# Two recurrent chains rebuilt: output sums of all heads in one PSUM bank, weights in groups of 160 columns, padded memory keys, short waits filled with products

## The chip, the cores and the metric

One core of one Trainium2 chip. The metric is the device time of one execution in microseconds (us). The engines: PE multiplies matrices and adds up in PSUM; DVE (vector), ACT (scalar) and POOL copy and compute; SP only issues transfers (DMA), as POOL does too; SBUF is the memory on the chip. Engines wait for each other by semaphores, counters that a finished instruction or transfer raises.

## The reference

The kernel computes the forward pass and all gradients of a gated mix of two blocks. Block A (multi-query attention) isn't touched. Block B is an attention that carries a memory: 64 segments of 32 tokens, each with 8 memory rows in front, 32 heads of 128; the outputs of the memory rows are the next segment's memory. Cut to what matters:

```python
for s in range(n_seg):                                   # 64, one after the other
    h = jnp.concatenate([mem, xs], axis=1)               # 8 memory rows + 32 tokens, 576 wide
    q, k, v = (jnp.einsum('btd,dhe->bhte', h, W) for W in (Wq, Wk, Wv))
    p = _softmax(where(mask, einsum('bhqe,bhke->bhqk', q, k) * scale, -1e9))
    o = jnp.einsum('bhqk,bhke->bhqe', p, v)
    o = jnp.einsum('bhte,hed->btd', o, Wo)               # sums over all heads
    mem = o[:, :M, :]                                    # the chain
    outs.append(o[:, M:, :])
out = g * a + (1 - g) * b                                # and the gradients by jax.vjp
```

The tokens' rows can be worked on 128 at a time. The memory rows can't: they make a forward chain of 64 segments and, for the gradient, a backward chain of 64.

## The kernel before

A segment of the forward chain, from the normalised outputs to the next memory:

```python
rl = sp.tile([P, 2, 1], F32, name="c_rl", bufs=2)
nc.vector.reciprocal(rl[:, :, 0], po[:, 2, 0:2])          # 256 reciprocals of the softmax sums
nc.vector.tensor_tensor(out=oc[:], in0=po[:, 0:2, :], in1=rl[:].to_broadcast([P, 2, P]), op=ALU.mult)
nc.gpsimd.dma_start(self.RL_m[s].rearrange("r p -> p r"), rl[:, :, 0])     # kept for the backward chain
# ... stores of ET, OM, ME, OT on POOL; transposes of oc; copy to oT ...
pw = psum.tile([P, 640], F32, name="c_pw", bufs=1)
for ri in range(8):                                       # 4 heads side by side: 64 products
    for lo, hi in ((0, 512), (512, D)):
        for g in range(4):
            self.mm(pw[32 * g:32 * g + 32, lo:hi], lhsT=oT[:, c0:c0 + 32], rhs=WoN[:, h, lo:hi],
                    start=(ri == 0), stop=(ri == 7), tp=(0, 32 * g))
ws = sp.tile([P, 640], F32, name="c_ws", bufs=1)          # two engines copy pw to ws, in f32
for kt in range(NKT):                                     # sum the 4 row groups, turn rows to columns
    self.mm(pm[:, kt, :], lhsT=ws[:, kt * P:(kt + 1) * P], rhs=self.selF[:, :], start=True, stop=True)
nc.vector.tensor_copy(mT[:, :, (s + 1) * MEM:(s + 2) * MEM], pm[:, :, :])
```

The backward chain has the same projection three times a segment (for v, k and q, with the transposed weights `WT`, 64 products each) and the same tail. `WT` is loaded before the backward chain and serves the x gradients too.

The softmax here doesn't subtract the row's maximum and nothing guards it: scores larger than these inputs give would overflow.

## Time and profile before

| | us | clock |
|---|---|---|
| time, median of 3 runs | 11834.84 (11804.16 to 11844.51) | 0.697 |
| forward chain | 1423 | 0.81 |
| x attention | 1510 | 0.77 |
| backward chain with its loads | 1150 | 0.88 |
| wait before the x gradients | 13 | |
| x gradients | 969 | 0.74 |
| memory rows | 118 | 0.51 |
| weight gradients | 687 | 1.00 |

The stages are cut at the first and last product of each on PE (the matmul engine); the first 5938 us (block A, projections, weight transposes) are left out. Clock is the mean share of full speed that PE was granted. The lines of the profile that carry this are in the prediction below.

### The profile page before, as it was taken

The page shows a single profiled execution, that of the slowest core. Times are in us where ns is not written, and L with a number is a line of the kernel's source. Part 1 is how long each engine was busy: PE and PEld are TensorE (multiplying, and loading weights), DVE is VectorE, ACT ScalarE, POOL GpSimd, SP SyncE. Part 2 cuts the span into 40 slices and gives each one's busy share as a digit, 9 for nine tenths or more (in the row PEclk, how much of TensorE's full clock was granted, in tenths as well). Part 3 has the DMA queues.
Part 4 walks back from the last instruction along what each step waited for, and adds up shares of the span by engine and source line. Part 5 has one row for each costly group of instructions (what it writes and reads, how often), then busy time and mean ns, then how long its engine had stood idle before and what let it go on. Part 6 is the DMA issues. An engine that isn't in the chain of part 4 may idle for free. (4 is left out here: it accounts for less than half of the span.)

```text
span 11807.0 us, 189310 instructions
## 1 busy us (share of the span) xinstructions
PE 10704.6 (91%) x79411; PEld 4101.3 (35%) x79798; DVE 4365.5 (37%) x6102; ACT 3510.0 (30%) x4681; POOL 2793.4 (24%) x5477
## 2 busy tenths in 40 slices
PE   7999999999999999989888888888887888999799
PEld 2212121212121212134433333555544554555444
DVE  4555555555555555534311111333332222122200
ACT  3444444444444444423311111222221111111100
POOL 3000000000000000013245555333334444333100
PEclk8555555555555555589888877777778988777799
DMA  2000000000000000045532222555544333555544
GB/s 66 1 4 1 4 1 4 1 4 1 4 1 1 4 1 1 1 144 231 201 83 54 54 55 70 190 174 167 176 152 149 90 93 94 186 188 187 192 147 145
DMA packets 583499, 980.07 MB, mean 83 GB/s; under 512 B 213801, under 2 KB 392114, under 8 KB 564402
## 3 DMA queue, kind: packets, MB, share of 16 engines
q1 hardware_dynamic: 421506, 632.91, 16.9%
q0 software_dynamic: 159824, 333.70, 8.4%
q8 instruction: 624, 10.22, 0.4%
q14 instruction: 233, 1.91, 0.1%
q10 hardware_dynamic: 1312, 1.33, 0.0%
HBM read 542.17 MB, written 425.07 MB: 82 GB/s over the span
## 5 line engine op out<-in xcount | busy, mean ns | idle before, releaser
L1178 DVE TENSOR_TENSOR a_U<-a_w,a_E 128x1024 bf16<-128x1024 f32 x1024 | 1252.1, 1224 | 1131.5 <-ACT a_E L1176 1088.1
L1105 DVE TENSOR_TENSOR a_U<-a_w,a_E 128x1024 bf16<-128x1024 f32 x1024 | 1253.4, 1225 | 962.5 <-ACT a_E L1103 962.3
L1176 ACT ACTIVATE a_E<-a_w 128x1024 bf16<-128x1024 f32 x1024 | 1049.1, 1025 | 1375.6 <-PE a_w L66 1373.1
L1103 ACT ACTIVATE a_E<-a_w 128x1024 bf16<-128x1024 f32 x1024 | 1048.8, 1025 | 1179.5 <-PE a_w L66 1179.5
L66 PE MATMUL a_w<-a_kaug,a_qaug 19*128 19x512 bf16 x2048 | 901.7, 600 | 4.8 <-ACT a_E L1176 4.1
L66 PE MATMUL a_w<-a_vaugT,a_doaT 19*128 19x512 bf16 x2048 | 836.0, 620 | 22.0 <-DVE a_U L1178 16.1
L66 PE MATMUL a_acc<-a_E,a_dog 128*32 128x512 bf16 x2048 | 625.0, 600 | 71.8 <-ACT a_E L1176 0.2
L66 PE MATMUL a_w<-a_doT,a_vaugT 19*128 19x512 bf16 x2048 | 670.8, 623 | 5.2 <-ACT a_E L1103 4.0
L66 PE MATMUL a_w<-a_qaug,a_kaug 19*128 19x512 bf16 x2048 | 658.0, 599 | 3.6 <-ACT a_doT L63 3.0
L1137 POOL TENSOR_TENSOR a_otok<-a_tk,a_rl 128x144 bf16<-128x144 f32 x64 | 27.4, 428 | 2570.8 <-DVE a_rl L1136 2570.8
L66 PE MATMUL a_acc<-a_U,a_ku 128*32 128x512 bf16 x2048 | 625.3, 607 | 0.2
L66 PE MATMUL a_acc<-a_U,a_qtok 128*32 128x512 bf16 x2048 | 623.1, 606 | 0.6 <-DVE a_U L1178 0.6
L66 PE MATMUL w_acc<-w_col,w_h 128*128 128x512 bf16 (+1 forms) x2352 | 523.4, 381 | 13.5 <-DMA w_col<-dqx 10.8
L1081 POOL DMA_DIRECT2D a_dog<-do_dram x8 | 4.7, 589 | 1814.1 <-PE a_acc L66 1810.0
L61 DVE CAST p_tok<-p_pb 128x512 bf16<-128x512 f32 x384 | 265.4, 692 | 318.4 <-PE p_pb L66 318.4
L66 PEld LDWEIGHTS <-a_qaug 19*128 19x128 bf16 x2048 | 152.2, 98 | 655.5 <-issue 655.5
L66 PE MATMUL a_acc<-a_E,a_evB 128*64 128x512 bf16 x1024 | 325.6, 612 | 54.0 <-ACT a_E L1103 0.6
L66 PEld LDWEIGHTS <-w_h 128*128 128x128 bf16 (+1 forms) x2400 | 237.4, 100 | 299.6 <-issue 34.3
L66 PEld LDWEIGHTS <-a_dog 128*32 128x32 bf16 x2048 | 108.9, 100 | 652.4 <-issue 652.2
L63 ACT COPY p_em<-p_tr 128x512 bf16<-128x512 bf16 x384 | 225.0, 586 | 357.8 <-PE p_tr L71 357.6
L66 PEld LDWEIGHTS <-d_g 128*32 128x32 bf16 x12288 | 271.4, 104 | 170.8 <-issue 60.7
L66 PEld LDWEIGHTS <-a_ku 128*32 128x32 bf16 x2048 | 105.9, 101 | 639.3 <-issue 639.2
(476 smaller groups left out, 16390.7 us busy)
## 6 DMA issues: line engine op xcount, KB each, us to landing
xt_k<-p_tok SPq DMA_DIRECT2D x16, 1024.0 KB
xe_k<-p_em POOLq DMA_DIRECT2D x16, 1024.0 KB
xs_k<-p_seg POOLq DMA_DIRECT2D x64, 256.0 KB
xt_v<-p_tok SPq DMA_DIRECT2D x16, 1024.0 KB
xe_v<-p_em POOLq DMA_DIRECT2D x16, 1024.0 KB
xs_v<-p_seg POOLq DMA_DIRECT2D x64, 256.0 KB
xt_q<-p_tok SPq DMA_DIRECT2D x16, 1024.0 KB
xe_q<-p_em POOLq DMA_DIRECT2D x16, 1024.0 KB
```

What stands on the lines that cost most here:

```text
L61: nc.vector.tensor_copy(out, in_)
L63: nc.scalar.copy(out, in_)
L66: return self.nc.tensor.matmul(out, lhsT, rhs, start=start, stop=stop, tile_position=tp, skip_group_check=True)
L1081: nc.gpsimd.dma_start(dog[:, :, :], self.do_dram[g])
L1103: nc.scalar.activation(ex[:], s[:], ACT.Exp, scale=SCALEA)
L1105: nc.vector.tensor_tensor(out=u[:], in0=d[:], in1=ex[:], op=ALU.mult)
L1137: nc.gpsimd.tensor_tensor(out=osl, in0=v[:, :, :, o0:o0 + DA], in1=rl[:].to_broadcast([P, 4, 2, DA]), op=ALU.mult)
L1176: nc.scalar.activation(ex[:], s[:], ACT.Exp, scale=SCALEA)
L1178: nc.vector.tensor_tensor(out=u[:], in0=d[:], in1=ex[:], op=ALU.mult)
```

## The change

The intent is to shorten a segment. (1) The output projection puts 160 columns on each of four column groups of the array (128 columns and 32 of the last 64), so that all 32 heads add up in one place and no sum over row groups in f32 is needed. (2) In the forward chain the memory keys are padded to 32 columns a head and v is used as it comes. (3) "Fills", products whose result nobody reads, are put into the short waits to keep PE's clock up. (4) Stores move from POOL to SP. Around these: weights are loaded in the grouped form, the backward chain recomputes the memory scores, `WT` is loaded after the backward chain, and some token forms are made by transposes instead of loads. The core of the diff:

```diff
+    def busy(self, pf, n, rhs):
+        w = rhs.shape[-1]
+        for _ in range(n):
+            self.mm(pf[0:32, 0:w], lhsT=self.identB[:, 0:32], rhs=rhs)
+    def load_160(self, t, src):
+        for h in range(0, HB, 8):
+            hs = slice(h, h + 8)
+            for j in range(4):
+                self.nc.sync.dma_start(t[:, hs, j, 0:P], src[:, hs, j * P:(j + 1) * P])
+                lo = 512 + 32 * (j % 2)
+                self.nc.sync.dma_start(t[:, hs, j, P:160], src[:, hs, lo:lo + 32])
 ... forward chain
-                nc.gpsimd.dma_start(self.RL_m[s].rearrange("r p -> p r"), rl[:, :, 0])
+                nc.sync.dma_start(self.RL_m[s].rearrange("(r p) -> p r", r=2), rl[:, :, 0])
+            self.busy(pf, 4, oc[:].rearrange("p r n -> p (r n)"))
-            pw = psum.tile([P, 640], F32, name="c_pw", bufs=1)
+            pw = psum.tile([P, 160], F32, name="c_S", bufs=1)
             for ri in range(8):
-                for lo, hi in ((0, 512), (512, D)):
-                    for g in range(4):
+                for g in range(4):
+                    for j in range(4):
+                        self.mm(pw[32 * j:32 * j + 32, :], lhsT=mEw(3, c0, c0 + 32), rhs=Wo160[:, h, j, :],
+                                start=(ri + g == 0), stop=(ri + g == 10), tp=(0, 32 * j))
+            self.rows_to_columns(...)        # two bf16 copies, 5 transposes, 1 copy, 3 fills
 ... backward chain: three such projections of 128 products in place of 64
+            W160[w] = wp.tile([P, HB, 4, 160], BF16, name=f"W160{w}")
+            self.load_160(W160[w], self.WT_dram[wi].rearrange("p (h d) -> p h d", d=D))
 ... main
+            with SB("p4o") as p4o, SB("p4s") as p4s, PS("p4p") as p4p:
+                k.b_chain_bwd(bk, p4o, p4s, p4p)
             with SB("p4w") as p4w:
                 k.load_WT(p4w)
-                with SB("p4o") as p4o, SB("p4s") as p4s, PS("p4p") as p4p:
-                    k.b_chain_bwd(bk, p4o, p4s, p4p)
```

## The prediction

> **What bounds the kernel now.** I read the mean clock first (one core, 0.697), then the whole span by stage, then single segments of the two chains on the timeline of the matmul engine, then the load queue. The chain that ended last covers only the last 6% of the span, the weight gradients, which the change leaves alone, so each stage has to be read by itself. The view of busy time by stage, cut at the stages' borders (attention of A; projections; weight transposes; forward chain; x attention; loads; backward chain; x gradients; memory rows; weight gradients):
> ```profile
> 0.00:5233.00 5233.00, 4919.38 (x18707) 1080.64 (x18731) 2725.66 (x2610) 2251.24 (x2293) 300.50 (x996) 0.53 0.03 10
> ...
> 5937.00:7359.00 1422.00, 1232.24 (x15734) 534.94 (x15734) 279.86 (x670) 217.23 (x479) 769.54 (x1338) 0.81 0.24 59
> 7359.00:8850.00 1491.00, 1259.96 (x11017) 752.47 (x11144) 500.62 (x1034) 423.64 (x759) 555.52 (x896) 0.77 0.53 174
> 8850.00:8915.00 65.00, 15.64 (x167) 9.88 (x167) 6.40 (x12) 7.48 (x13) 17.81 (x33) 0.60 0.73 292
> 8915.00:10021.00 1106.00, 954.54 (x18817) 566.86 (x18817) 279.09 (x672) 119.49 (x288) 515.17 (x1005) 0.89 0.32 93
> 10021.00:11003.00 982.00, 949.10 (x7102) 503.08 (x7199) 190.33 (x448) 161.87 (x288) 326.18 (x736) 0.74 0.58 183
> ```
> Columns: stretch, its length, busy time (and count) of PE, weight loads, DVE, ACT, POOL, then granted clock, DMA share, GB/s. The change can win in the two chains, 1422 and 1106 us; attention of A, 5233 us, is untouched. Both chains are PE's: 64 segments, each waiting for the last one's state. The forward chain runs at clock 0.81, the backward one at 0.89.
>
> A forward segment takes 22.30 us (mean of 63 start-to-start distances of its first product), 18.74 us in the one that ran wholly at full clock. The PE timeline of one tail and the next start:
> ```profile
> 6621.62 2.14 PE L66 MATMUL c_pw<-WoN,c_oT 128*32 128x512 bf16 x64 [0.45 <-DVE c_oT L311]
> 6624.43 1.28 PE L66 MATMUL c_o<-selF,c_ws 128*128 128x8 f32 x10 [0.67 <-DVE c_ws L324]
> 6626.01 1.05 PE L66 MATMUL c_pb<-Wq,c_mT 128*32 128x512 bf16 x16 [0.29 <-DVE c_mT L330]
> 6626.98 0.62 PE L66 MATMUL c_pb<-Wqk,c_mT 64*32 64x512 bf16 x4
> 6627.53 1.90 PE L66 MATMUL c_pb<-Wq,c_mT 128*32 128x512 bf16 x16
> ```
> The reader is to see three things: ten f32 passes of 1.28 us between two copies; the brackets, which are PE standing still; and the same 16 products taking 1.05 us, then 1.90 us: the clock fell by half at about 6627.0 and came back at 6630.4, after 3.4 us. The idle brackets before the output transposes, selF, pw, the v product and the next q sum to 161 us over the chain; the clock costs more: 22.30 - 18.74 = 3.56 us a segment, 224 us.
>
> **What the skill says.** "TensorE: Matmul & The Clock Gate", Part 1: the clock halves after an idle window of about 3.4 us, windows run freely, and only half and full rate exist. The trace agrees: a cold stretch of 3.4 us, and .427 against .213 us for a 512-column step.[...] The same page, "Wait — 56ns, not 53.3ns?": starts never closer than some 25 ns however small N is. The trace agrees for full-width weights (25 ns for 32-column products in the backward scores), but four 32-column tiles side by side do better: sixteen in .23 us, 14.6 ns each (second to first start below, 128 columns each). "TensorEngine Tiling (Array Packing)", Key Properties: a change of tiling mode drains the engine; here each switch shows as about .11 us (the 64-row step takes .33 instead of .21 us). "DMA: Bandwidth & Descriptors", Specifications: pieces under 512 B don't reach line rate; no transfer of before resembles the new one, so the trace neither agrees nor disagrees.
> ```profile
> 10434.17 0.41 PE L66 MATMUL x_p<-g_ke,g_me 128*32 128x128 bf16 x16
> 10434.40 0.40 PE L66 MATMUL x_p<-g_ve,g_mde 128*32 128x128 bf16 x16
> ```
>
> **Forward chain.** Steps of the full-clock segment: q, k, v up to the scores 10.0; scores to sums 1.16; sums to v product 1.06; to the output transposes 1.45; to pw .67; pw to selF 2.81; selF to next q 1.58; sum 18.7. After: q, k, v unchanged, 10.0. Scores: 16 pairs of 32 columns at 25 ns, with two fills, 1.25. The copy of v back to token form leaves the path (2 transposes, a copy: 1.06) because v's rows now serve as padded values; sums, products and copies to the output transposes 1.45, with the four fills (.85) inside the reciprocal and multiply (.17 + .42 and their latencies). To pw .70. pw: 32 groups of four tiles of 160 columns at about .070 (160/128 of .0585) = 2.2 against 2.0. Tail: two copies .5, five transposes .2, one copy .2 and their waits 1.45, where two f32 copies, ten f32 passes and one copy took 2.3. Sum 17.1. If the fills hold the clock, every segment is near it: (22.30 - 17.1) x 63 = 328, less some cold windows: **-315 us**, of which 1.6 x 63 = 100 is structure and the rest is clock. Stores moved from POOL to SP lie beside.
>
> For the fills: single narrow products, 18 columns wide, held full clock through two windows:
> ```profile
> 91.25 5.15 PE L66 MATMUL a_p<-a_xT,a_wkv 128*18 128x512 bf16 x20 [0.22 <-DVE a_kt L61]
> 97.06 2.60 PE L66 MATMUL a_p<-a_xT,a_wkv 128*18 128x512 bf16 x10 [0.66 <-ACT a_vt L63]
> ```
> .26 us each, not .43. Against: attention of A is 94% PE-busy at clock 0.53, with products of 19 rows, so busy time alone isn't what counts. The fills use all 128 rows.
>
> **Backward chain.** Mean 17.08 us, all-warm segment 15.48. Removed: f32 passes and two larger copies of the tail (2.3 to 2.6 becomes 1.4, -1.0), and half of the score multiply before the first transpose (-.3). Added: recomputed scores (.3, partly inside the projections), a multiply by an f32 row instead of a copy (+.15), fills, three projections at 2.2 instead of 2.0 (+.6, but part of the v one now fills waits: -.3). Clock 0.89 to about .97: -.6. Sum -1.15 x 63 = **-70 us**.
>
> **Elsewhere.** The queue before:
> ```profile
> 8874.45 2.33 SPq L601 DMA_DIRECT2D WTq<-wt_d  x4
> 8876.82 2.02 SPq L601 DMA_DIRECT2D WTk<-wt_d  x4
> 8879.77 9.72 SPq L601 DMA_DIRECT2D WTv<-wt_d  x4
> 8892.21 12.01 SPq L611 DMA_DIRECT2D WoTb<-wot_d  x5
> ```
> Weights now come in 32,768 pieces of 256 and 64 B each; over 16 engines 2048 pieces apiece. I estimate 16 to 25 ns a piece, so 33 to 52 us per weight. Forward: one weight, +25 us before the first segment's projection. Backward: three, 100 to 150 us, against about 45 us for WT and WoTb (19 MB at 420 GB/s): +75. WT (14 MB, 34 us at that rate) is loaded after the chain, ahead of the x gradients: +36. Memory rows: 16 groups instead of 12 at about 7.0 us: +28. X attention: two more groups of four transposes and copies in each of 32 halves, 85% PE-busy, about .6 each: +20. X gradients: 97% PE-busy, eight transposes and sixteen 128-column products more, .8 a half: +26. Masks: POOL's 128 selects for maskC (26 us, ahead of a gradient load for which PE and DVE wait) become 64 and some memsets: -12.
>
> **Sum**: -315 - 70 - 12 + 25 + 75 + 36 + 28 + 20 + 26 = -187; I take -205, since some of the added work will lie in waits. 11,835 - 205 = **11,630 us**, -1.7%.
>
> **Rivals.** (a) The fills don't hold the clock: 32 columns may count as a quarter. For: stage A's 0.53. Against: the 18-column products. Then only structure stays (-100, -35) and the overheads win: about 11,880. (b) The small pieces are slower than estimated, 40 ns each: four weights at 80 us, +150: about 11,780. For: the skill's line-rate remark. (c) Groups of four 160-column tiles are bound by issue at 25 ns: 3.2 instead of 2.2 us, one forward and three backward projections: +63 + 189, and the backward chain gets slower: about 11,880. Against: 14.6 ns above. (d) Loads and transposes hide, and the backward chain reaches full clock with its waits filled: about 11,480.
>
> **Range and chances.** The chains' gain may be 300 to 460, the overheads 120 to 270; the error of the sum is some 120 us. Range 11,480 to 11,790. Two per cent faster is below 11,598, just beyond my centre: 0.41; slower by two per cent needs (a) and (b) together: 0.03; within: 0.56.
>
> **What would show it.** Forward segments near 17.2 us at clock above .95 (right), or near 20.5 at .8 (a); pw of 128 products at 2.2 us or 3.2 (c); backward segments near 15.9; PE idle before the first projections of both chains and before the x gradients of 25, 75 and 36 us; 16 memory-row groups. The prediction is wrong if any of the three big terms (clock forward, loads, projections) misses by half.

## The result and the profile after

12295.41 us, median of 4 runs (12290.36 to 12324.1), against 11822.02 us of the kernel before (also 4 runs): a ratio of 1.0404, 95% interval 1.0378 to 1.0431. It is slower by 4%, where 1.7% faster was predicted. Executions over 1.5% slower than the fastest of the same kernel are left out of the means. A ratio is the mean time of one kernel's fast runs over that of the other's of the same rounds, so it isn't quite the ratio of the medians quoted.

By stage, cut at the same products, from the profiled runs (11807.0 and 12288.6 us):

| stage | before | after | difference | predicted |
|---|---|---|---|---|
| up to the forward chain | 5937.7 | 5931.7 | -6 | -12 |
| forward chain | 1423.0 | 1561.1 | +138 | -290 |
| x attention | 1509.6 | 1562.4 | +53 | +20 |
| backward chain with its loads | 1149.9 | 1392.0 | +242 | +5 |
| wait before the x gradients | 12.8 | 44.7 | +32 | +36 |
| x gradients | 969.4 | 965.2 | -4 | +26 |
| memory rows | 118.0 | 145.1 | +27 | +28 |
| weight gradients | 686.6 | 686.4 | 0 | 0 |

The two chains miss by 428 and 237 us; all the rest by less than 40 each. The busy time by stage after, in the columns that the prediction explains:

```profile
5931.00:7492.00 1561.00, 1238.09 (x20923) 556.03 (x20923) 264.89 (x638) 223.59 (x448) 33.20 (x128) 0.87 0.19 41
...
9055.00:9172.00 117.00, 8.78 (x50) 2.10 (x49) 0.69 (x1) 1.17 (x2) 0.72 (x3) 0.50 1.13 193
9172.00:10447.00 1275.00, 1066.76 (x31633) 701.63 (x31632) 234.09 (x606) 170.25 (x415) 7.69 (x62) 0.99 0.27 78
```

The clock rose, to 0.87 (above 0.95 was predicted) and 0.99 (about 0.97), and the chains got longer all the same. The counts show what else grew: in the backward chain PE now runs 31633 products, before 18817, each with a weight load of its own. The waits for loads came about as predicted. These three PE lines stand where PE waited (the bracket is the wait and what ended it; on SP's queue the transfer named stands behind the weights):

```profile
5969.79 0.21 PE L66 MATMUL c_S<-c_mE,c_kx 128*128 128x32 bf16 x1 [24.52 <-DMA c_kx<-xs_k]
9171.82 0.40 PE L66 MATMUL d_g<-d_mE 128*128 128x128 bf16 x2 [92.95 <-DMA d_mE<-me]
10491.83 0.66 PE L66 MATMUL x_b<-WTq,g_dqe 128*128 128x512 bf16 x2 [44.08 <-DMA g_dqe<-dqe]
```

**Backward chain.** A segment now takes 19.64 us (median; 17.26 before). The PE timeline of a segment's projections:

```profile
9616.04 1.29 PE L66 MATMUL d_pw<-W160v,d_g 128*32 128x160 bf16 x64
9617.16 1.75 PE L66 MATMUL d_pw<-W160k,d_g 128*32 128x160 bf16 x89
9620.24 0.87 PE L66 MATMUL d_pw<-W160k,d_g 128*32 128x160 bf16 x39 [1.33 <-issue]
9620.88 1.75 PE L66 MATMUL d_pw<-W160q,d_g 128*32 128x160 bf16 x89
9624.26 0.87 PE L66 MATMUL d_pw<-W160q,d_g 128*32 128x160 bf16 x39 [1.62 <-issue]
9624.90 0.59 PE L66 MATMUL d_pf<-d_g,identB 128*32 128x512 bf16 x2
```

In the middle of a row of like products, whose data are all there, PE stops for 1.33 and 1.62 us with no releaser ("issue"). Between the two stops lie 39 + 89 = 128 products and as many weight loads: 256 instructions. Counted in the trace, all 120 stops in this chain where two products start over 1.2 us apart (first segment left out) come after the same number modulo 256 of PE instructions. The view of PE's waits for nearly the whole backward chain (total us, times, longest):

```profile
PE d_pw L66 <- issue: 189.8, 135, 2.5
```

The profile's page lists an instruction queue, whose transfers are of 16 KB, 64 bytes for each of 256 instructions. In this chain each took 1.10 us in the mean and none over 2 us, so they aren't slow. Each of the 120 stops ends 1.1 to 1.6 us after such a block has arrived. In the dense stretches from 9602 to 9700 us blocks start 3.3 to 4.3 us apart, while PE, when it has instructions, gets through 128 pairs in 2.2 us.

**Forward chain.** A segment takes 24.03 us in the mean (22.14 before, first segment left out). The PE timeline of a tail, and one line of ACT from the timeline of all engines:

```profile
6214.92 2.40 PE L66 MATMUL c_S<-Wo,c_mE 128*32 128x160 bf16 x128
6217.15 0.59 PE L66 MATMUL c_pf<-c_mE,identB 128*32 128x512 bf16 x2
6223.05 0.21 PE L343 MATMUL c_tr<-identB,c_ws 32*32 32x32 bf16 x4 [5.31 <-ACT c_ws L337]
...
6224.38 1.90 PE L66 MATMUL c_pb<-Wq,c_mT 128*32 128x512 bf16 x16
```
```profile
6222.81 0.18 ACT L337 CAST c_ws<-c_S 128x32 bf16<-128x32 f32 x1 [9.78 <-remote]
```

The projection takes the predicted 2.2 us. Then PE waits 5.31 us for a copy of ACT, and ACT waits for PE's semaphore that tells that the projection is done, which the trace records only at 6222.79. Everything is late at once: the instruction block that started at 6217.34 took 6.68 us, and no recorded semaphore at all moved from 6215.7 to 6219.7. After that wait the clock is at half (1.90 us for the 16 q products). Where two products start over 1.2 us apart I call it a pause and count its time above 0.3 us: 70 pauses with 286 us in the forward chain, none before. They stand at many places (before the turning of `c_ws`, the transposes of `c_tm`, inside the projection), so no single wait of the program explains them. Nor are most of them tied to instruction blocks as in the backward chain: only 13 of the 70 share a remainder modulo 256 (105 or 106), and PE resumes anywhere from before the end of the last block's transfer to 14 us after it. The row of the instruction queue for the forward chain, before and then after (transfers, MB, share of the time of 16 engines):

```profile
q8 instruction: 113, 1.85, 0.9%
```
```profile
q8 instruction: 150, 2.46, 1.4%
```

0.9% of 16 x 1300 us over 113 is 1.7 us a block; 1.4% of 16 x 1400 over 150 is 2.1 us. The trace's single transfers give 2.08 us in the mean, 7.65 at the longest, 51 of 160 over 2 us.

### The profile page after: what moved, and what is told of

Its sections match the earlier page's. It is cut to its first block, busy times and chain, and to the rows that moved or that the text cites. A ratio compares the mean times of both kernels' runs of the same rounds, so it can differ in the third digit from the quotient of the medians.

```text
span 12288.6 us, 224497 instructions
## 1 busy us (share of the span) xinstructions
PE 10906.5 (89%) x98614; PEld 4326.7 (35%) x99000; DVE 4303.2 (35%) x5990; ACT 3608.7 (29%) x4858; POOL 1251.5 (10%) x2893
## 3 DMA queue, kind: packets, MB, share of 16 engines
q10 hardware_dynamic: 1312, 1.33, 0.0%
## 5 line engine op out<-in xcount | busy, mean ns | idle before, releaser
L66 PEld LDWEIGHTS <-d_g 128*32 128x32 bf16 x24576 | 430.9, 97 | 240.9 <-issue 221.6
L66 PEld LDWEIGHTS <-c_mT 128*32 128x32 bf16 (+1 forms) x7680 | 178.8, 100 | 473.5 <-issue 349.6
L63 ACT CAST c_tm<-c_pb 128x512 bf16<-128x512 f32 x192 | 112.4, 585 | 750.6 <-PE c_pb L66 659.8
```

What stands on the lines that cost most here:

```text
L63: nc.scalar.copy(out, in_)
L66: return self.nc.tensor.matmul(out, lhsT, rhs, start=start, stop=stop, tile_position=tp, skip_group_check=True)
```

## The experiments

Theory I: PE runs out of instructions; in the backward chain because it asks for too many, in the forward chain because their blocks arrive late, held up by some transfer that the change moved. Rivals: order of the stores on SP's queue (II), 160-column groups dear by themselves (III), an unseen wait for data (IV). Theory I took another form after the first four runs. "Whole" times are medians; ratios are to the kernel before.

| run | us | ratio | forward: segment, pauses | backward: segment |
|---|---|---|---|---|
| before (profiled) | 11808.8 | | 22.14, 0 | 17.26 |
| after | 12295.4 | 1.0404 | 24.03, 286 | 19.64 |
| f_rl_pool | 12295.8 | 1.0400 | 24.32, 301 | 19.74 |
| b_half_instr (wrong numbers) | 12053.7 | 1.0195 | 24.14, 297 | 16.18 |
| no_fills | 12255.2 | 1.0366 | 24.79, 291 | 18.70 |
| before_split (wrong numbers) | 11899.1 | 1.0064 | 22.14, 4 | 17.94 |
| f_rl_end | 11852.9 | 1.0013 | 17.24, 0 | 19.65 |
| f_stores_pool | 12193.8 | 1.0301 | 22.75, 225 | 19.78 |
| b_oldproj | 11950.9 | 1.0096 | 23.60, 267 | 17.00 |
| win1 | 11493.2 | 0.9710 | 17.25, 0 | 15.18 |
| f_end_nofills | 11762.3 | 0.9955 | 17.09, 0 | 18.68 |
| f_end_spread | 11842.8 | 1.0023 | 17.23, 0 | 19.60 |
| before_rl_end | 11819.6 | 1.0009 | 22.03, 0 | 17.40 |
| f_end_dense | 12246.4 | 1.0374 | 23.38, 261 | 19.64 |
| f_end_pitch64 | 11855.2 | 1.0043 | 17.27, 1 | 19.81 |
| win2 | 11467.5 | 0.9715 | 17.07, 0 | 15.18 |
| f_rl_last | 12230.6 | 1.0355 | 23.25, 249 | 19.61 |
| before_rl_sp | 11795.3 | 0.9986 | 21.60, 24 | 17.42 |

Forward segments are means without the first, backward ones medians (the first holds the load), both in us from the profiled run.

### b_half_instr: half the instructions for the same columns

```diff
-                for n in range(lo, hi):
+                for n in range(lo, hi, 2):
-                        self.mm(pw[32 * j:32 * j + 32, :], ..., rhs=W160[w][:, h, j, :],
+                        self.mm(pw[32 * j:32 * j + 32, :].rearrange("p (a n) -> p a n", a=2), ...,
+                                rhs=W160[w][:, h:h + 2, j, :],         # 320 columns; wrong numbers
```

> The changed kernel with the backward projections as 64 products of 320 columns instead of 128 of 160: the same column steps, half the instructions, wrong numbers on purpose. Theory I (PE takes 256 instructions in 2.2 us, and blocks of 256 come only every 3.3 to 4 us): the pauses without a releaser in the projections, 1.1 to 1.9 us each and 190 us over most of the chain, go; a segment falls from 19.7 to about 16 us; the whole about 12,060. Rival III (narrow groups or their weights cost that much by themselves, at an even rate): a projection gets shorter evenly and the pauses were never single events; Rival IV (the pauses are waits for a transfer or buffer of the chain): unchanged, about 12,290.

12053.7 us. The numbers are wrong as intended (0.70 relative error in one output). The PE timeline of the same place, and the wait that is left of the 189.8 us, from the view of PE's waits over the same chain:

```profile
9505.33 1.27 PE L66 MATMUL d_pw<-W160v,d_g 128*32 128x320 bf16 x32
9506.42 2.35 PE L66 MATMUL d_pw<-W160k,d_g 128*32 128x320 bf16 x64
9508.60 2.35 PE L66 MATMUL d_pw<-W160q,d_g 128*32 128x320 bf16 x64
```
```profile
PE d_pw L66 <- issue: 1.0, 5, 0.3
```

A projection without a pause still takes 2.2 us, which is the time of its columns; but the pauses are gone, and the segment falls by 3.46 us to 16.18. III and IV fall. Weight loads are halved too; it is the period of 256 instructions, above, that speaks for the supply of instructions and not for the cost of a weight load.

### before_split: more instructions in the kernel that had no pauses

```diff
-                    for lo, hi in ((0, 512), (512, D)):
+                    for lo, hi in ((0, 256), (256, 512), (512, D)):    # backward projections only
```

> The kernel before, with each 512-column product of its backward projections cut in two of 256: 96 products per projection instead of 64 for the same columns, right results. Theory I: PE now asks for 256 instructions in some 2.8 us, pauses without a releaser appear in a chain that had none, 1 to 2 us per segment, and the time rises by 60 to 150 us. If only the 160-column form is at fault: no pauses, the time within 30 us of before.

11899.1 us, +0.6%. Contrary to what I had written the numbers are wrong (0.23 in one output); I didn't trace why. The view of PE's waits over the backward chain has a line that the kernel before doesn't have:

```profile
PE d_pw L66 <- issue: 50.5, 57, 2.0
```

The same columns in 96 instead of 64 products make the pauses appear with the plain weights too. The whole is 75 us longer, of 60 to 150 expected; a segment 0.7 us (17.94 against 17.26), less than the 1 to 2 expected. So the kernel before stood about at the limit: 64 pairs in 2.1 us, some 16 ns an instruction, while blocks of 256 every 3.3 to 4.3 us give 13 to 17.

### f_rl_pool: the reciprocals' store on its old queue

```diff
-                nc.sync.dma_start(self.RL_m[s].rearrange("(r p) -> p r", r=2), rl[:, :, 0])
+                nc.gpsimd.dma_start(self.RL_m[s].rearrange("(r p) -> p r", r=2), rl[:, :, 0])
```

> The changed kernel with one store of the forward chain, the 256 reciprocals of 4 bytes each, issued by POOL (software queue) again instead of SP. Theory I (instruction blocks of 16 KB arrive late in the forward chain because they share the transfer engines with the 4-byte pieces that now go through the hardware queue): blocks back near 1.1 us each instead of 2.1 mean and 7.7 longest, the forward chain's pauses (286 us above the normal) fall to under 100, segments from 23.3 to about 19 us, the whole about 12,050. Rival II (the pauses come from the order of loads and stores on SP, or from the other two stores): no change beyond 40 us, about 12,280.

12295.8 us, no change, 301 us of pauses. My first form of the theory, that the queue made the difference, fell.

### f_stores_pool and f_rl_last: the order on SP

```diff
-            nc.sync.dma_start(...)      # ET_m, RL_m, ME, forward chain
+            nc.gpsimd.dma_start(...)
```

> The changed kernel with all three stores of the forward chain (exponentials, reciprocals, memory states) issued by POOL instead of SP. Theory I, mended: the 4-byte pieces remain, so no change beyond 60 us. Rival II (the order of loads and stores on SP's queue makes the pauses): pauses from 286 us to under 80, the whole about 12,050.

12193.8 us; 225 of 286 us of pauses stay. And the store of the reciprocals moved behind the large one on the same queue:

```diff
-            nc.sync.dma_start(self.RL_m[s]...)      # ahead of the transposes of oc
             nc.sync.dma_start(self.ME[s]...)
+            nc.sync.dma_start(self.RL_m[s]...)
```

> The changed kernel with the packed store of reciprocals issued after the 256 KB store of the memory states instead of before it. If the packed store does its harm to what queues behind it: pauses fall from 286 us to under 150, the whole about 12,100. If it holds up all traffic wherever it stands: within 40 us of 12,295.

12230.6 us, 249 us of pauses. Both help a little (102 and 65 us of the whole, outside what either case of their expectations allowed), but most of the pauses stay: neither queue nor order is the main cause.

### f_rl_end: no small stores in the chain

The reciprocals stay in SBUF through the chain; at its end one product with an f32 identity turns them, and one store writes them in rows of 512 bytes.

```diff
+        rlall = sp.tile([P, NSEG, 2, 1], F32, name="c_rlall", bufs=1)
-            rl = sp.tile([P, 2, 1], F32, name="c_rl", bufs=2)
+            rl = rlall[:, s]
-                nc.sync.dma_start(self.RL_m[s].rearrange("(r p) -> p r", r=2), rl[:, :, 0])
+        self.mm(prl[:, 0, :], lhsT=rlall[:].rearrange("p s r o -> p (s r o)"), rhs=self.identF[:, :])
+        nc.vector.tensor_copy(rlT[:], prl[:, 0, :])
+        nc.sync.dma_start(self.RL_m.rearrange("s (r p) -> (s r) p", r=2), rlT[:])
```

> The changed kernel with the reciprocals kept on the chip through the forward chain, turned by one product at its end and stored once in rows of 512 bytes, so that no segment stores 256 pieces of 4 bytes; right results. Theory I, mended (the queue doesn't matter, the 4-byte writes themselves hold up every later transfer for some 5 us, instruction blocks and semaphore counts among them): blocks back to about 1.1 us, pauses over 1.2 us in the forward chain from 286 us to under 60, segments about 18 us instead of 24, the whole about 11,980. Rival V (the pauses come from the 256 KB store and the loads issued beside it, whatever the reciprocals do): pauses stay near 286 us, the whole near 12,290.

11852.9 us, 442 less than the changed kernel, correct. The same tail, and the row of the instruction queue for the chain:

```profile
6212.17 2.40 PE L66 MATMUL c_S<-Wo,c_mE 128*32 128x160 bf16 x128
6214.39 0.59 PE L66 MATMUL c_pf<-c_mE,identB 128*32 128x512 bf16 x2
6214.92 0.20 PE L354 MATMUL c_tr<-identB,c_ws 32*32 32x32 bf16 x4
...
6215.87 1.05 PE L66 MATMUL c_pb<-Wq,c_mT 128*32 128x512 bf16 x16
```
```profile
q8 instruction: 155, 2.54, 1.0%
```

From projection to next q 3.7 us instead of 9.5. No pause is left, a block takes 1.09 us (1.0% of 16 x 1040 us over 155), none over 2, and the segment is 17.2 us, which was the prediction's sum of 17.1. The stage goes from 1561 to 1134 us. One store of 1 KB a segment had cost 427.

### f_end_dense, f_end_pitch64, f_end_spread: what about that store

On top of f_rl_end, a copy of the reciprocals that nobody reads is stored in every segment to a fresh tensor; only the distance of its 256 pieces of 4 bytes differs: 4, 64 and 512 bytes.

```diff
+        self.SCR = DT([NSEG, 256], "scr", F32)            # dense; [NSEG, 256, 16] and [NSEG, 256, 128]
+                nc.sync.dma_start(self.SCR[s].rearrange("(r p) -> p r", r=2), rl[:, :, 0])   # or SCR[s][:, 0]
```

> The changed kernel with one store of the reciprocals at the end, and beside it in each segment a copy that nobody reads: the same 256 pieces of 4 bytes on SP's queue, but each 512 bytes from the next instead of in one kilobyte. If it is the size of the pieces that holds up the transfers: pauses again near 286 us, the whole near 12,290. If it is that many pieces fall in the same few lines of memory: pauses under 60 us, the whole near 11,870.

> Control for the spread copy: the same never-read copy of 256 pieces of 4 bytes in each segment, to a fresh tensor too, but packed in one kilobyte. If the packing is the cause: pauses over 1.2 us near 286 us in all, instruction blocks of 4 us and more, the whole near 12,290. If it was the old tensor's place in memory: no pauses, near 11,850.

> The same copy with the pieces 64 bytes apart, 16 KB in all. If what counts is that pieces share one line of 64 bytes or less: no pauses, near 11,850. If it is a wider stretch of memory that they crowd: some of the pauses, 50 to 286 us.

Dense 12246.4 us with 261 us of pauses; 64 bytes apart 11855.2; 512 apart 11842.8. PE's longest waits in the forward chain, dense and then 64 bytes apart:

```profile
PE c_tr L357 <- ACT c_ws L351: 78.2, 15, 7.2
PE c_S L66 <- issue: 67.7, 23, 7.2
```
```profile
PE c_S L66 <- issue: 1.7, 2, 1.4
```

So it is neither the number of pieces nor their size nor that tensor's place in memory: 256 pieces of 4 bytes do no harm when each has 64 bytes to itself, and cost 390 us (12246 - 11855) when they are packed.

### no_fills and f_end_nofills: what the fills are worth

```diff
-        for _ in range(n):
+        for _ in range(0):
             self.mm(pf[0:32, 0:w], lhsT=self.identB[:, 0:32], rhs=rhs)
```

> The changed kernel without its filling products in both chains. If fills hold the clock as I predicted: the forward clock falls from 0.87 to about 0.80 and the backward one from 1.00 to about 0.9, and the time rises by some 50 to 150 us. If they do nothing: clocks unchanged, and the time falls by up to 60 us because the fills' own time leaves the path.

> The changed kernel with one store of the reciprocals at the end, and without the filling products of both chains. With the pauses gone this shows what fills are worth: if they hold the clock, a forward segment goes from 17.2 back to 18.5 to 20 us at a clock of 0.85 to 0.9, and the whole is 80 to 200 us above the run with fills (11,853). If they don't, it is 17.2 or less and the whole 11,800 to 11,850.

With the pauses there, the clock of the forward chain falls to 0.81 without fills, as expected, and the time falls too, by 40 us. By stage (profiled runs) the two chains part: the forward chain takes 1610 us without fills, against 1533 to 1574 in after, b_half_instr and b_oldproj, whose forward code is the same; the backward chain with its loads falls from 1392 to 1326 us. So in the changed kernel the forward fills did help. Without the pauses, busy time by stage over the same stretch of the forward chain, without fills and then with them:

```profile
6000.00:7030.00 1030.00, 913.42 (x19052) 458.89 (x19052) 249.88 (x602) 205.77 (x425) 31.63 (x121) 0.98 0.18 52
```
```profile
6000.00:7030.00 1030.00, 1025.86 (x19684) 499.07 (x19681) 247.49 (x597) 209.10 (x419) 31.22 (x120) 1.00 0.17 52
```

The clock is 0.98 without a single fill. The rest of the change, its shorter waits most likely, is enough to keep it; the fills bring PE from 89 to 100% busy and lengthen the median segment from 16.78 to 17.20 us. In the backward chain a segment falls from 19.65 to 18.68 us without them. The whole is 11762.3 us, 80 less than f_end_spread, which has the fills and no forward pauses either. By stage, 66 of the 80 lie in the backward chain (1387 to 1320 us; clock 0.99 to 0.96), which in both runs is still short of instructions and where each fill is two more of them (waits for instructions 183 us with fills, 154 without); only 10 lie in the forward chain (1134 to 1123 us). What a fill costs where instructions are not short is shown by the forward chain alone.

### before_rl_end and before_rl_sp: why the kernel before wasn't hurt

```diff
-                nc.gpsimd.dma_start(self.RL_m[s].rearrange("r p -> p r"), rl[:, :, 0])
+                ...                                      # as f_rl_end; or the same line with nc.sync
```

> The kernel before with nothing changed but this: its reciprocals are kept through the forward chain, turned once and stored once. In it an instruction block took up to 3.4 us, but no pause above 1.2 us is seen. If the small writes cost it only what shows as pauses: within 30 us of before. If they slow its POOL stores and with them its copies and its clock: a segment from 22.1 to about 20.5 us, the whole 60 to 150 us faster.

> The kernel before with its packed store of reciprocals on SP's queue, the one other thing that the change did to it. If the hardware queue makes it harmful where PE's load is that of before: pauses over 1.2 us appear in the forward chain and the time rises by 50 to 300 us. If before is immune because of its lower rate of instructions and of its other transfers: no pauses, within 30 us.

Without the packed store its blocks fall from 1.58 to 1.09 us, but the time stays (ratio 1.0009, interval 0.9992 to 1.0025): there was no pause to win back. With the store on SP 14 pauses with 24 us appear, blocks take up to 5.5 us instead of 3.4, and the time doesn't rise (0.9986 from 2 runs, interval 0.9951 to 1.0022). So the packed store delays blocks in the kernel before as well, less, and PE there takes fewer of them: 119 in the forward chain against 160.

### b_oldproj, win1, win2: repairs

b_oldproj gives the backward chain its old projections, weights and f32 tail and takes its fills out; the rest of the change stays. win1 is b_oldproj with that tail in bf16, and f_rl_end. win2 is win1 without the fills of the forward chain.

```diff
-                    for j in range(4):
-                        self.mm(pw[32 * j:32 * j + 32, :], ..., rhs=W160[w][:, h, j, :], ...)
+                for ri in range(lo // 4, hi // 4):
+                    for a, b in ((0, 512), (512, D)):
+                        for g in range(4):
+                            self.mm(pw[32 * g:32 * g + 32, a:b], ..., rhs=self.WT[w][:, h, a:b], ...)
-            self.rows_to_columns(sp, psum, "d", pw, ...)
+            ...                                          # tail of before; ws and selF bf16 in win1, win2
```

> The changed kernel with the backward projections, their weights and their tail of before (64 products a projection, plain weights kept over the x gradients) and without fills there; right results. Instruction supply theory: the pauses of the backward chain go, a segment falls from 19.7 to about 16.5 us, the 93 us wait for the grouped weights falls to about 30 and the 54 us wait before the x gradients to about 12: together about 300 us, the whole about 11,990. If the backward loss came from the other parts of its rewrite (the recomputed scores, the stores on SP): less than 150 us.

> Both repairs together, with the backward tail in bf16: the forward chain's new form without the 4-byte stores, the backward chain's old projections; right results. If both theories hold the gains add up: about 12,295 - 310 - 320 = 11,665 us, 1.3% faster than before. If the forward theory fails: about 11,975, slower than before.

> The combined repair without the filling products of the forward chain. From the two runs of the repaired forward chain with and without fills (17.20 and 16.78 us a segment) 63 x 0.42 = 26 us less than with them: about 11,465 us, 3% faster than before.

b_oldproj is 345 us below the changed kernel: its backward stage falls by 263 us and the wait before the x gradients by 33; the rest is in the forward chain (28) and the x attention (12), whose code is the same: that much the profiles of one code differ while the packed store is in. win1 is correct and takes 11493.2 us, much less than the 11,665 expected: the gains of b_oldproj (345) and f_rl_end (442) add up. win2 is correct and takes 11467.5 us, 2.85% faster than before (ratio 0.9715, interval 0.9698 to 0.9731). The 26 us that it was to gain on win1 are not shown: its time came out as expected, but the kernel before ran 34 us faster in that call, and win1's ratio was 0.9710. Its chains in the view by stage:

```profile
5929.00:7048.00 1119.00, 969.59 (x20095) 484.68 (x20088) 265.25 (x639) 216.62 (x447) 33.25 (x128) 0.97 0.20 57
...
8645.00:9657.00 1012.00, 866.96 (x18686) 452.61 (x18678) 257.30 (x733) 177.72 (x416) 7.71 (x62) 0.95 0.34 101
```

1119 us instead of 1423, and 1012 against 1106, with 18686 backward products where the changed kernel had 31633.

## Why the prediction was wrong

- **The step that failed, backward chain:** "three projections at 2.2 instead of 2.0 (+.6 ...)". The 2.2 us was right for a burst of 128 products and false for three in a row: PE's instructions come in blocks of 256, and three projections need three blocks in 6.6 us. The pauses cost 190 us (3.5 us a segment by b_half_instr). Rival (c) had the right place and the wrong mechanism: not every product was slower, the stream stopped. That its +189 us meets the 190 is luck.
- **The step that failed, forward chain:** "Stores moved from POOL to SP lie beside." One of the stores, 1 KB in 256 packed pieces, held up instruction blocks and semaphores, 286 us of pauses and then 141 us more (427 - 286, taken as a remainder), which the half clock seen after pauses (0.87 instead of 1.00) may explain; no run takes it apart. The move itself was harmless; the store was harmful in the new chain on either queue. Its own sum of 17.1 us was right once that store was gone (17.2).
- **Right number, wrong reason:** "If the fills hold the clock". Without the packed store the forward clock is 0.98 with no fill at all, and the chain is 10 us shorter. My evidence that narrow products hold the clock was beside the question; the rest of the change, its shorter waits most likely, had already answered it. Only where the packed store opened longer waits did the fills hold the clock (0.87 against 0.81).
- **Read too simply:** "the clock halves after an idle window ... The trace agrees". The trace shows a fixed grid of 3.41 us, but in the forward chain of the kernel before (first segment left out) 65 of these windows lost the clock with PE 54 to 83% busy by the trace and never idle for more than 0.74 us, while 27 windows at 65 to 67% kept it. What a fill has to lift was thus not known.
- **Right:** the grouped weights at the forward start (25 predicted, 24.5 measured) and before the backward chain (+75; from the end of the x attention to the end of the wait for loads 45 us before, 117 after, +72; to the first projection 64 and 122, +58). The 16 to 25 ns a piece behind both had no measurement to rest on, so that they came out is partly luck. Also `WT` after the chain (+36, +32), memory rows (+28, +27). **Mis-sized:** x attention, +53 for +20, and x gradients, -4 for +26; no run here takes these apart.
- The backward segment without pauses is 16.18 us, with fills, against the predicted 15.9: but for the supply of instructions the sum there was right.
- The range failed because every rival was a variation of one picture, PE limited by columns, issue, clock or data. That the instructions themselves have to be brought in was not in it, though the profile's page lists their queue and the count of products could be read off the diff. The Trainium skill, "Runtime: NRT & Kernel Launch", section "Instruction fetch mechanics", says that instructions come in blocks of 16 KB, which this trace agrees with, and that the fetch is hidden because dispatch is slower than the filling; here it isn't (189.8 us). I hadn't read that page before I predicted.

Left open: how packed small writes delay PE's semaphores and the blocks, and why the same store does so little in the kernel before; that packing is what matters is shown, the mechanism is not. Open too is why blocks that take 1.1 us each start only every 3.3 to 4.3 us while PE waits for them.

## What to carry to other kernels

Count PE's instructions, not only its columns: here stretches that took 256 of them in clearly less than 3.5 us for several blocks (2.2 us, some 2.7 in before_split) stopped, and fewer, wider products were worth more than a shorter tail. Store small results in rows, once, after a loop; if small pieces have to be written inside it, give each 64 bytes of its own, the smallest distance tried here that did no harm. Before filling waits to hold the clock, look whether the clock falls without the fills.

## What the Trainium skill lacked or had wrong

- "Runtime: NRT & Kernel Launch", Instruction fetch mechanics: the claim that the fetch is hidden doesn't hold for weight-load and product pairs of 17 ns. Blocks of 256 started 3.3 to 4.3 us apart in the dense stretches; 189.8 us of pauses in one chain, 1.0 with half the instructions.
- "DMA: Bandwidth & Descriptors": it warns of pieces under 512 bytes, and of stalled writes that stall other queues only for transfers between cores; not that small packed pieces written to DRAM delay other traffic. 256 pieces of 4 bytes in 1 KB delayed instruction blocks from 1.1 us to as much as 8.1 and cost 390 us in 64 segments; the same pieces 64 bytes apart cost nothing visible (11855.2 against 11852.9 us).
- "TensorE: Matmul & The Clock Gate": nothing on products put into a kernel's waits only to keep the clock up. In the forward chain they raised it from 0.98 to 1.00 and cost 10 us; with the packed store's pauses they raised it from 0.81 to 0.87 and saved time (1533 to 1574 us against 1610).
